# Output products of a retention and two-feed-forward kernel by seven block products, product by product over all feature rows of 768 tokens, with weight sums read back from DRAM

## The chip, the cores and the metric

The kernel runs on one core of a Trainium2 chip. The metric is the device time of one execution in microseconds. The median of three runs of the kernel before is 873.28 us (871.96 to 876.17). TensorE (PE) does the matrix products, VectorE (DVE) and ScalarE (ACT) the elementwise work, GpSimd (POOL) a little at the start, and SyncE (SP) issues every DMA, in the order of the program, on one queue.

## The reference, cut to what matters

```python
def _attn_ref(q, k, v):                      # (4, 8, 576, 64) each
    scores = scale * np.matmul(q, k.transpose(0, 1, 3, 2))
    ...
    return np.matmul(scores * Dmat[None, :, :, :], v)      # Dmat: gamma ** (i - j), i >= j
def _moe_ref(x, w_in, w_out):                # x (2304, 512), w_in (512, 2048), w_out (2048, 512)
    h = x @ w_in
    g = np.maximum(h, 0.0) + np.log1p(np.exp(-np.abs(h)))
    return g @ w_out
def _moe2_ref(x, w_in, w_out):               # same shapes
    h = x @ w_in
    r = np.maximum(h, 0.0)
    return (r * r) @ w_out
# reference: x = _attn_ref(q, k, v) as (2304, 512); x = _moe_ref(x, moe weights); _moe2_ref(x, moe2 weights)
```

Everything is float32. The kernel splits each operand of a product into a high and a low part of a shorter type (fp32r) and adds three products: high by high, low by high, high by low.

## The kernel before, in words

**First phase.** Attention runs in chunks of 64 tokens; its output is the input of the first feed-forward part, in five token tiles (TILES: 512, 384, 512, 512, 384 tokens). For each tile there are 16 steps f, one for each 128 rows of the hidden features: `g1` (L424) makes the hidden product in 12 matmuls, `softplus_a` and `softplus_b` and `split_g` make the activation and its two parts on ACT and DVE, `g2` (L476), two steps later, adds 12 matmuls into four accumulators. The result is stored to DRAM (`x2d`). Beside it `pump_step` takes weights through a chain: load, decode (`words`), split. First come the 32 weight tiles of this phase, then `split_s`: for each of 8 pairs p of the second part's input weights it makes seven block sums (two parts each) and stores them to DRAM (`s2d`) by four calls of `store_s`. That is nine steps a pair, 72 in all, spread over tiles 1 to 3. The second part's output weights (16 tiles, `split_w`) stay in SBUF; they are pumped in the last tile and the start of the second phase.

**Second phase.** Three blocks b of 768 tokens, each in two halves of 384. For a pair p of hidden row blocks the hidden product is made by seven block products (Winograd's form of Strassen's scheme): `product` (L568) makes each in 6 matmuls of 384 columns, its weights from a ring of five slots that one DMA of 256 KB each fills from `s2d`. The sums s1, u2, u3 and the four results are taken from PSUM by ACT and DVE between products; `finish` squares the positive part and splits it. The output products are plain: `piece` (L587) takes 128 tokens and one hidden row block in 3 matmuls of 512 columns, and six accumulators gather them over all pairs. `after(k)` puts one or two pieces behind each product, so each evacuation of a product's PSUM has the pieces and the next product beside it.

A tile scheduler sets the order on each engine from these calls; it may move an instruction ahead of others that don't depend on it.

Of the kernel before, what the change touches and what calls it, by code (L numbers as in the profile page):

```python
# [7 lines left out]
F32 = mybir.dt.float32  # L8
# [25 lines left out]
T_SLOTS = 10  # L34
S_SLOTS = 5
# [7 lines left out]
def kernel(  # L43
# [66 lines left out]
    s2d = dram.tile([NP, 7, P, 2, KH * P], F32, name="s2d")  # L110

# [66 lines left out]
    def store_s(p, first, src):  # L178

        n = src.shape[1] // (KH * P)  # L180
        h, l = (new_ct(F32R)[:, :n * KH * P] for _ in range(2))
        nc.scalar.copy(h, src)
        nc.vector.tensor_tensor(out=l, in0=src, in1=h, op=ALU.subtract)
        for part, o in enumerate((h, l)):
            nc.sync.dma_start(
                out=s2d[p, first:first + n, :, part].rearrange("o p c -> p o c"),
                in_=o.bitcast(F32).rearrange("p (o c) -> p o c", o=n),
            )

    def split_s(p):  # L190
# [9 lines left out]
        store_s(p, A11, top)  # L200
        yield
        store_s(p, A22, a22)
# [7 lines left out]
        store_s(p, S3, bot)  # L210
        yield
        store_s(p, S2, top)
# [17 lines left out]
    order = [f for p in range(NP // 2) for f in (p,)] + [NP, NP + 1]  # L230
    for p in range(2, NP):
        order += [p + NP] + ([p + 2] if p < NP - 2 else [])
    for f in order:
        items.append((1, split_w, (1, "wo", f)))
        loads.append((w2_out, "wo", f))
# [262 lines left out]
    def second_buffers():  # L498

        for i in range(LOADS):  # L500
            mem["ch", i] = at.tile([P, 4, HALF], F32, tag="ch", name="raw")
        mem["s"] = xs.tile([P, 4, 2, KH * P], F32R, tag="xr", name="sring")
        mem["s4"] = cvt.tile([P, 2, KH * P], F32R, tag="ct", name="sring")
# [8 lines left out]
    def s_slot(i):  # L512
        i %= S_SLOTS
        if i < 4:
            return mem["s"][:, i]
        return mem["s4"]
# [10 lines left out]
    n_s = [0]  # L527

    def load_s(upto):
        total = NB * NP * 7  # L530
        while n_s[0] < min(upto, total):
            i = n_s[0]
            nc.sync.dma_start(out=s_slot(i).bitcast(F32), in_=s2d[i // 7 % NP, PRODUCTS[i % 7]])
            n_s[0] += 1
# [24 lines left out]
    def product(b, p, k, ps, first):  # L559

        w = s_slot((b * NP + p) * 7 + k)
# [11 lines left out]
    pieces = []  # L573
    acc2 = {}

    def piece(b, p, i, j, m, g):

        h, l = g
        f = p + i * NP
        wh, wl = w_hi[1, "wo", f], w_lo[1, "wo", f]  # L580
        begin, end = p == 0 and i == j, p == NP - 1 and i != j
        if begin:
            pool, tag = (((ps_acc, "at"),) * 4 + ((ps_at, "at"), (ps_st, "st")))[j * MH + m]
            acc2[j, m] = pool.tile([P, 512], F32, tag=tag, name="acc")
        c = slice(m * P, (m + 1) * P)
# [4 lines left out]
        if end:  # L590
            t0 = b * PAIR + j * HALF + m * P
            drain_one(j * MH + m, acc2[j, m], out[t0:t0 + P, :], DM)

    n_g = [0]

    def finish(b, p, i, j, c, done=None):

        if done is None:
            g = ew.tile([P, 512], F32, tag="l", name="g")[:, :HALF]
            nc.vector.scalar_tensor_tensor(  # L600
                out=g, in0=c, scalar=0.0, in1=c, op0=ALU.max, op1=ALU.mult
            )
        else:
            g = ew.tile([P, 512], F32, tag="l", name="g")[:, :HALF]
            nc.vector.tensor_tensor(out=g, in0=done, in1=done, op=ALU.mult)
        k = n_g[0] % 4
        n_g[0] += 1
        if k < 2:
            h = gp.tile([P, 512], F32R, tag="gh", name="gh")[:, :HALF]
            l = gp.tile([P, 512], F32R, tag="gl", name="gl")[:, :HALF]  # L610
        else:
            h, l = (mem["g"][:, 2 * (k - 2) + o, :HALF] for o in range(2))
        nc.scalar.copy(h, g)  # L613
        nc.vector.tensor_tensor(out=l, in0=g, in1=h, op=ALU.subtract)
        for m in range(MH):
            pieces.append((b, p, i, j, m, (h, l)))

    def second_phase(rest):

        mem["g"] = xs.tile([P, KD, 512], F32R, tag="xh", name="gring")  # L620
        mem["u"] = xs.tile([P, KD, 512], F32, tag="xl", name="uring")
        u_ring = mem["u"].rearrange("p a b -> p (a b)")
        n_u = 0

        count = (2, 2, 2, 1, 2, 2, 1)
        skip = 5
        for b in range(NB):
            for p in range(NP):
# [5 lines left out]
                def after(k):  # L634
# [5 lines left out]
                    elif b == p == 0 and k < skip:  # L640
                        pass
                    else:
                        for _ in range(count[k]):
                            piece(*pieces.pop(0))
                    if p == 0 and k in (0, 1) and b + 1 < NB and k == 1:
                        load_raw(b + 1)
                    if b + 1 < NB and p in (3, 4, 5) and k == 2:
                        build_t((b + 1) * 7 + p - 3)
                    if b + 1 < NB and p == NP - 1 and k < 4:
                        build_t((b + 1) * 7 + 3 + k)  # L650
                    if b == 0 and k in (0, 3):
                        if n_split[0] < len(items) and not (p >= 4 and k == 3):
                            pump(1)
                    load_s((b * NP + p) * 7 + k + 1 + S_SLOTS)

                def add(a, ps):
                    c = ew.tile([P, 512], F32, tag="e", name="c", bufs=3)[:, :HALF]
                    nc.vector.tensor_tensor(out=c, in0=a, in1=ps, op=ALU.add)
                    return c

                px = h_bank("px")[:, :HALF]
# [3 lines left out]
                py = h_bank("py")[:, :HALF]  # L665
# [4 lines left out]
                r = ew.tile([P, 512], F32, tag="e", name="r", bufs=3)[:, :HALF]  # L670
                nc.scalar.activation(out=r, in_=px, func=AF.Relu)
                later.append(lambda: finish(b, p, 0, 0, None, r))
# [4 lines left out]
                pz = h_bank("pz")[:, :HALF]  # L677
                product(b, p, 4, pz, True)
                c22 = add(u3, pz)
                later.append(lambda: finish(b, p, 1, 1, c22))  # L680
                after(4)
                product(b, p, 5, py, False)
                c21 = add(s1, py)
                later.append(lambda: finish(b, p, 1, 0, c21))
                after(5)
                product(b, p, 6, pz, False)
                c12 = add(u2, pz)
                later.append(lambda: finish(b, p, 0, 1, c12))
                after(6)
        while pieces:  # L690
            piece(*pieces.pop(0))
# [116 lines left out]
    for j, (b, f) in enumerate(steps):  # L808
# [15 lines left out]
        if 1 <= b < last_b:  # L824

            total, i = 9 * NP, (b - 1) * KF + f
            while n_steps[0] < min(total, -(-total * (i + 1) // (KF * (last_b - 1) - 2))):
                pump_step()
                n_steps[0] += 1
        if b == last_b:  # L830
            if f == 0:
                assert n_split[0] == n_one + NP and not splitting
                second_buffers()
                load_raw(0)
                load_s(S_SLOTS)
            if f >= 4 and f % 2 == 0:
                pump(1)
# [6 lines left out]
    split_g(j - 1, TILES[last_b][1])  # L844
    second_phase([lambda: g2_parts(j - 2), lambda: g2_parts(j - 1)])
# [75 lines left out]
```

## Time and profile before

| | before |
|---|---|
| median of 3 runs | 873.28 us |
| profiled execution | 873.51 us |
| its span, first to last instruction | 871.7 us |
| PE, PEld (weight load), DVE, ACT busy | 852.1, 745.1, 585.0, 427.0 us |
| mean granted TensorE clock, share of 2.4 GHz | 0.989 |
| DMA | 126.34 MB, mean 145 GB/s |

The profile's page gives busy time by engine. A matmul's end is modelled and matmuls overlap, so the time that one takes in a row of them is the distance of two starts, which the chain of waits shows as the length of a piece divided by its count. The chain of waits follows the end back from wait to wait; the list of waits tells who waited for whom.

### The profile page before, as it was taken

The numbers are of one execution on the slowest core, as the hardware profiler recorded it, in microseconds if no ns is written. First come the engines' busy times: TensorE is split into PE (matmuls) and PEld (weight loads), VectorE is DVE, ScalarE is ACT, GpSimd is POOL, SyncE is SP. The second block draws the span as 40 slices with busy tenths as digits, with TensorE's granted clock in tenths as the row PEclk, the third lists the DMA queues.
The fourth block names the chain that finished last, engine by engine and source line by source line (L and its number), as shares of the span: only waits on it lengthen the run. The fifth ranks groups of instructions, "written<-read, shape, count | busy, mean of one in ns | idle before, by whom it ended". The sixth has DMA issues, their size and how long they took to land.

```text
span 871.7 us, 14325 instructions
## 1 busy us (share of the span) xinstructions
PE 852.1 (98%) x5520; PEld 745.1 (85%) x5520; DVE 585.0 (67%) x1038; ACT 427.0 (49%) x795; POOL 9.3 (1%) x12
## 2 busy tenths in 40 slices
PE   8899999999999999999999999999999999999998
PEld 6677787989888888788999989889888988998996
DVE  4689998986897578755888874446745446554444
ACT  3589998665676456744686561213312113221121
POOL 2100000000000000000000000000000000000000
PEclk9699999999999999999999999999999999999999
DMA  8856774972394116710431464436644444644342
GB/s 206 219 165 201 217 207 113 286 240 53 95 293 132 39 49 222 233 43 1 169 115 55 145 230 121 119 112 193 192 114 117 121 117 116 191 119 114 118 121 85
DMA packets 75784, 126.34 MB, mean 145 GB/s; under 512 B 6722, under 2 KB 41666, under 8 KB 75714
## 3 DMA queue, kind: packets, MB, share of 16 engines
q1 hardware_dynamic: 75716, 125.42, 49.1%
q8 instruction: 44, 0.72, 0.4%
q14 instruction: 24, 0.20, 0.1%
HBM read 101.28 MB, written 24.12 MB: 144 GB/s over the span
## 4 chain that ended last, share of the span: by engine, by line
PE 79%; DVE 7%; DMA 6%; ACT 4%; issue 2%; SPq 1%; POOL 0%; DVEq 0%; ACTq 0%
PE acc L587 23%; PE ph L424 16%; PE acc L476 16%; PE py L568 9%; PE px L568 6%; PE pz L568 6%; DMA ch<-in_kv_dram 2%; DMA wo_raw<-in_moe_w_out_dram 2%; PE po L359 2%; PE pb L330 1%; DMA s2d<-ct 1%; DVE e L451 1%; DVE l L448 1%; PE st L336 1%; DVE ct L145 1%
## 5 line engine op out<-in xcount | busy, mean ns | idle before, releaser
L424 PE MATMUL ph<-xh,wi 128*128 128x512 f32 (+1 forms) x640 | 146.0, 369 | 2.3 <-DVE e L451 1.3
L424 PEld LDWEIGHTS ph<-xh,wi 128*128 128x128 f32 x640 | 116.3, 188 | 19.8 <-DVE e L451 2.4
L476 PE MATMUL acc<-gh,woh 128*128 128x512 f32 (+1 forms) x320 | 120.2, 379 | 0.7 <-ACT gh L460 0.7
L476 PE MATMUL acc<-gh,wol 128*128 128x512 f32 (+1 forms) x320 | 118.1, 369 | 0.0
L476 PE MATMUL acc<-gl,woh 128*128 128x512 f32 (+1 forms) x320 | 117.9, 369 | 0.0
L587 PE MATMUL acc<-woh,gring 128*128 128x512 f32 x288 | 104.9, 393 | 0.0
L568 PE MATMUL py<-t,sring 128*128 128x384 f32 x432 | 86.8, 335 | 0.3 <-DVE uring L675 0.3
L568 PEld LDWEIGHTS py<-t,sring 128*128 128x128 f32 x432 | 77.2, 188 | 6.8 <-DVE uring L675 0.6
L460 ACT CAST gh<-e 128x512 fp32r<-128x512 f32 (+1 forms) x80 | 46.0, 575 | 73.3 <-DVE e L451 65.7
L424 PE MATMUL ph<-xl,wi 128*128 128x512 f32 (+1 forms) x320 | 78.7, 367 | 0.0
L445 DVE SCALAR_TENSOR_TENSOR e<-e 128x512 f32<-128x512 f32 (+1 forms) x80 | 50.9, 637 | 33.8 <-ACT l L440 32.8
L461 DVE TENSOR_TENSOR gl<-e,gh 128x512 fp32r<-128x512 f32 (+1 forms) x80 | 51.0, 637 | 31.2 <-ACT gh L460 30.5
L476 PEld LDWEIGHTS acc<-gh,woh 128*128 128x128 f32 x320 | 59.8, 188 | 9.4 <-ACT gh L460 0.8
L613 ACT CAST gh<-g 128x384 fp32r<-128x384 f32 x48 | 24.6, 513 | 87.1 <-DVE g L600 72.4
L476 PEld LDWEIGHTS acc<-gh,wol 128*128 128x128 f32 x320 | 60.1, 188 | 7.9
L476 PEld LDWEIGHTS acc<-gl,woh 128*128 128x128 f32 x320 | 60.1, 188 | 7.2 <-DVE gl L461 0.2
L613 ACT CAST gring<-g 128x384 fp32r<-128x384 f32 x48 | 24.6, 513 | 83.4 <-DVE g L600 83.4
L424 PEld LDWEIGHTS ph<-xl,wi 128*128 128x128 f32 x320 | 58.7, 188 | 7.6
L587 PEld LDWEIGHTS acc<-woh,gring 128*128 128x128 f32 x288 | 54.0, 188 | 9.2
L438 ACT ACTIVATE e<-ph 128x512 f32<-128x512 f32 (+1 forms) x80 | 44.2, 552 | 33.2 <-PE ph L424 32.7
L568 PE MATMUL px<-t,sring 128*128 128x384 f32 x288 | 58.3, 337 | 0.0
L568 PE MATMUL pz<-t,sring 128*128 128x384 f32 x288 | 58.2, 337 | 0.0
(79 smaller groups left out, 1458.4 us busy)
## 6 DMA issues: line engine op xcount, KB each, us to landing
sring<-s2d SPq DMA_DIRECT2D x168, 256.0 KB, 2.7
wi_raw<-in_moe_w_in_dram SPq DMA_DIRECT2D x32, 512.0 KB, 4.5
wo_raw<-in_moe_w_out_dram SPq DMA_DIRECT2D x32, 512.0 KB, 4.6
s2d<-ct SPq DMA_DIRECT2D x48, 256.0 KB, 3.1
ch<-in_qk_t_dram SPq DMA_DIRECT2D x36, 256.0 KB, 4.6
ch<-in_kv_dram SPq DMA_DIRECT2D x36, 256.0 KB, 4.9
raw<-x2d SPq DMA_DIRECT2D x12, 384.0 KB, 3.3
out_dram<-xo SPq DMA_DIRECT2D x18, 256.0 KB, 2.2
```

What stands on the lines that cost most here:

```text
L145: nc.vector.scalar_tensor_tensor(out=ct, in0=up, scalar=3, in1=low, op0=ALU.logical_shift_left, op1=ALU.bitwise_or,)
L330: nc.tensor.matmul(pb[to, h, :], lhsT=kk[LO, hh, :], rhs=qp[LO, hh, :], start=True, stop=True, skip_group_check=True,)
L359: nc.tensor.matmul(po[(LO, HI)[h % 2], h // 2, :], lhsT=sv[rows, h, :], rhs=qp[rows, h, :], start=True, stop=True, skip_group_check=True,)
L424: nc.tensor.matmul(ph[:, :n], lhsT=a, rhs=x, start=(j == 0), stop=(j == len(todo) - 1))
L438: nc.scalar.activation(out=e, in_=ph[:, :n], func=AF.Abs)
L445: nc.vector.scalar_tensor_tensor(out=e, in0=e, scalar=-2.0, in1=e, op0=ALU.add, op1=ALU.mult)
L460: nc.scalar.copy(h[:, :n], g)
L461: nc.vector.tensor_tensor(out=l[:, :n], in0=g, in1=h[:, :n], op=ALU.subtract)
L476: nc.tensor.matmul(acc[j][:, :n], lhsT=a, rhs=x, start=(begin and m == 0), stop=(end and m == 2))
L568: nc.tensor.matmul(ps, lhsT=a, rhs=x, start=(first and m == 0), stop=(m == len(todo) - 1), skip_group_check=True,)
L587: nc.tensor.matmul(acc2[j, m], lhsT=a, rhs=x, start=(begin and n == 0), stop=(end and n == 2))
L613: nc.scalar.copy(h, g)
```

## The change

The second phase's output products are made by seven block products too. The 768 tokens by 2048 features of a block are one operand, the 16 output weight tiles the other; the blocks are the two token halves, the feature halves (p and p + 8) and the two halves of the 512 outputs. A block b now runs in two parts. First come all hidden products of the eight pairs, one behind the other, each evacuated into a buffer for all features (`g_slot`, in the space of the first phase's weights). Then come 56 units, product by product over all eight p: `split_unit` makes the operand (a sum or difference on DVE for four of the seven products) and its two parts three units ahead (AHEAD), `unit` runs 9 matmuls of 256 columns, and after the eighth unit of a product its sum is taken from PSUM.

The output weights' sums are made in the first phase by `split_o` (eight pairs, nine steps each) and stored to a new DRAM tensor `o2d`. The steps of both splits, 144, are spread over tiles 1 to 4 instead of 72 over tiles 1 to 3. The ring has ten slots; each unit loads one 256 KB tile from `o2d`, as each product does from `s2d`.

```diff
-T_SLOTS = 10
-S_SLOTS = 5
+T_SLOTS = 8
+S_SLOTS = 10
+AHEAD = 3
+O_PRODUCTS = (0, 3, 1, 4, 6, 2, 5)
...
+    def split_o(p):
+        cts = []
+        for f in (p, p + NP):
+            t = staged.pop(("wo", f))
+            cts.append(new_ct())
+            yield from words(t, cts[-1])
...
+        store_s(o2d, p, 0, a11)
+        yield
+        store_s(o2d, p, 1, bot)
+        yield
+        nc.vector.tensor_tensor(out=a22, in0=a21, in1=a22, op=ALU.add)
...
+        store_s(o2d, p, 3, top)
+        yield
+        store_s(o2d, p, 5, bot)
+        yield True
...
-    for f in order:
-        items.append((1, split_w, (1, "wo", f)))
-        loads.append((w2_out, "wo", f))
+    for p in range(NP):
+        items.append((2, split_o, (p,)))
+        loads += [(w2_out, "wo", p), (w2_out, "wo", p + NP)]
...
+        in_order += [s2d[p, k] for p in range(NP) for k in PRODUCTS]
+        in_order += [o2d[p, k] for k in O_PRODUCTS for p in range(NP)]
...
-        for n, (a, x) in enumerate([(h[:, c], wh), (h[:, c], wl), (l[:, c], wh)]):
-            nc.tensor.matmul(
-                acc2[j, m], lhsT=a, rhs=x, start=(begin and n == 0), stop=(end and n == 2)
-            )
...
+    def split_unit(u):
+        k, p = units[u]
+        g11, g12, g21, g22 = (g_slot(p, i, j) for i in range(2) for j in range(2))
+        t2 = g_extra(p)
+        if k == 1:
+            minus(t2, g22, g11)
+        elif k == 5:
+            minus(g21, g21, t2)
+        src = (g11, t2, g21, g12, g11, g21, g22)[k]
...
+        nc.scalar.copy(h, src)
+        minus(l, src, h)
+        if k == 0:
+            minus(g11, g12, g11)
+        elif k == 2:
+            minus(g12, g22, g12)
+        pairs[u] = h, l
...
+        for m in range(MH):
+            c = slice(m * P, (m + 1) * P)
+            for n, (a, x) in enumerate([(h[:, c], w[:, 0]), (h[:, c], w[:, 1]), (l[:, c], w[:, 0])]):
+                nc.tensor.matmul(
+                    blocks[m], lhsT=a, rhs=x, start=(first and p == n == 0 and m in opens),
+                    stop=(p == NP - 1 and n == 2), skip_group_check=True,
+                )
...
+            split_unit(u + AHEAD)
+            unit(b, u, blocks, tiles, k in where)
+            load_s((2 * b + 1) * NP * 7 + u + 1 + S_SLOTS)
...
-                    else:
-                        for _ in range(count[k]):
-                            piece(*pieces.pop(0))
...
-            total, i = 9 * NP, (b - 1) * KF + f
-            while n_steps[0] < min(total, -(-total * (i + 1) // (KF * (last_b - 1) - 2))):
+            total, i = 18 * NP, (b - 1) * KF + f
+            while n_steps[0] < min(total, -(-total * (i + 1) // (KF * last_b - 4))):
                 pump_step()
```

The order on PE in the second phase, before (px, py, pz are the PSUM tiles of the hidden products, t their operand, sring the weight ring; acc are the output accumulators, gh and gl or gring the two parts of the activation, woh and wol those of the output weights):

```order
L568 MATMUL px<-t_4821,sring 128x384 [waits DMAHW5_49,Activation_49]
L568 MATMUL px<-t_4821,sring 128x384 x5
L587 MATMUL acc<-woh_5493,gring 128x512
L587 MATMUL acc<-wol_5494,gring 128x512
L587 MATMUL acc<-woh_5493,gring 128x512 x2
L587 MATMUL acc<-wol_5494,gring 128x512
L587 MATMUL acc<-woh_5493,gring 128x512
L568 MATMUL py<-t_4821,sring 128x384 [waits DMAHW6_49,DVE_49]
```

The same place after, and two units of the second part (there px, py and pz are the sums of the output products):

```order
L613 MATMUL pz<-t_5219,sring 128x384 [waits DMAHW2_49]
L613 MATMUL pz<-t_5219,sring 128x384 x5
L613 MATMUL py<-t_5219,sring 128x384 [waits DMAHW3_49,DVE_49]
L613 MATMUL py<-t_5219,sring 128x384 x5
L613 MATMUL pz<-t_5348,sring 128x384 [waits DMAHW4_49,DVE_49]
```

```order
L678 MATMUL px<-sring,gh 128x256 [waits DMAHW5_49,Activation_49]
L678 MATMUL px<-sring,gh 128x256
L678 MATMUL px<-sring,gl 128x256 [waits DVE_49]
L678 MATMUL px<-sring,gh 128x256 x2
L678 MATMUL px<-sring,gl 128x256
L678 MATMUL px<-sring,gring 128x256 [waits DMAHW6_49,Activation_49]
```

The pieces no longer stand between the hidden products; one product of 6 matmuls stands between a product and the next one that writes the same PSUM tile, and a unit waits for a DMA, for ACT and for DVE.

The order on DVE at the last pair (p = 7) of a block's hidden products, before (L667 makes u2, L675 u3, L605 the square of the first result, L557 the low part of the next block's operand t):

```order
L614 TENSOR_TENSOR gring<-g,gring 128x384 [waits Activation_49]
L557 TENSOR_TENSOR t_4693<-raw,t_4693 128x768 [waits PE_49,Activation_49]
L667 TENSOR_TENSOR uring<-uring,py 128x384 [waits PE_49,Activation_49]
L557 TENSOR_TENSOR t_4693<-raw,t_4693 128x768 [waits Activation_49]
L557 TENSOR_TENSOR t_4821<-raw,t_4821 128x768 [waits PE_49,Activation_49]
L605 TENSOR_TENSOR g<-r 128x384 [waits Activation_49]
L675 TENSOR_TENSOR uring<-uring,py 128x384 [waits PE_49]
```

After (L791 makes u2, L797 u3, L778 the square, L602 the next block's operand, L767 a result):

```order
L602 TENSOR_TENSOR t_4926<-raw,t_4926 128x768 [waits PE_49,Activation_49]
L791 TENSOR_TENSOR uring<-uring,py 128x384 [waits PE_49,Activation_49]
L602 TENSOR_TENSOR t_4926<-raw,t_4926 128x768 [waits DMAHW4_49,Activation_49]
L602 TENSOR_TENSOR t_5078<-raw,t_5078 128x768 [waits PE_49,Activation_49]
L778 TENSOR_TENSOR g<-r 128x384 [waits Activation_49]
L797 TENSOR_TENSOR uring<-uring,py 128x384 [waits PE_49]
L602 TENSOR_TENSOR t_5078<-raw,t_5078 128x768 [waits Activation_49]
L767 TENSOR_TENSOR g<-uring,pz 128x384 [waits DVE_49,PE_49]
```

The builds of the next block stand in the same place, ahead of u2 and u3, while the pieces that stood beside them on PE are gone.

## Rows read from the trace of the kernel before

**Rows 1.** The page: busy us (share of the span) and instructions of each engine.
```profile
PE 852.1 (98%) x5520; PEld 745.1 (85%) x5520; DVE 585.0 (67%) x1038; ACT 427.0 (49%) x795; POOL 9.3 (1%) x12
```

**Rows 2.** Busy time by stretch: first phase's tiles 1 and 2, and the second phase.
```profile
core 0: us, PE busy (x) PEld busy (x) DVE busy (x) ACT busy (x) POOL busy (x), PEclk, DMA share, GB/s
138.00:222.30 84.30, 80.81 (x754) 75.97 (x753) 69.16 (x137) 54.99 (x111) 0.00 (x0) 1.00 0.55 164
222.30:319.80 97.50, 97.50 (x754) 79.85 (x753) 75.60 (x134) 59.30 (x105) 0.00 (x0) 1.00 0.45 130
...
740.00:862.00 122.00, 122.00 (x607) 109.55 (x606) 58.75 (x106) 24.67 (x49) 0.00 (x0) 1.00 0.43 121
```

**Rows 3.** The chain of waits in the second phase: start us, us, what.
```profile
642.09 1.06 PE px L568 x6
643.15 1.39 PE acc L587 x6
644.54 1.04 PE py L568 x6
...
861.01 4.14 PE acc L587 x18
```

**Rows 4.** Groups by shape on PE: count | busy us, mean ns | idle before, releaser.
```profile
L587 PE MATMUL acc<-woh,gring 128*128 128x512 f32 x288 | 104.9, 393 | 0.0
...
L568 PE MATMUL py<-t,sring 128*128 128x384 f32 x432 | 86.8, 335 | 0.3 <-DVE uring L675 0.3
...
L568 PEld LDWEIGHTS py<-t,sring 128*128 128x128 f32 x432 | 77.2, 188 | 6.8 <-DVE uring L675 0.6
```

**Rows 5.** Waits of PE from 138 to 482 us: us in total, times, longest.
```profile
PE pb L330 <- DVE e L451: 3.3, 5, 1.4
...
PE ph L424 <- DVE ch L341: 0.3, 1, 0.3
```

**Rows 6.** Timeline at 51.7 us, after a wait of PE: start us, us, instruction.
```profile
51.72 0.19 PEld L476 LDWEIGHTS acc<-gh,woh 128*128 128x128 f32 x1
51.73 0.50 PE L476 MATMUL acc<-gh,woh 128*128 128x512 f32 x1
51.83 0.19 PEld L476 LDWEIGHTS acc<-gl,woh 128*128 128x128 f32 x1
...
52.06 0.39 PE L476 MATMUL acc<-gl,woh 128*128 128x512 f32 x1
```

**Rows 7.** Timeline: a product's evacuation, PE's wait for one, two DVE operations.
```profile
707.13 1.21 PE L568 MATMUL py<-t,sring 128*128 128x384 f32 x6
...
708.44 0.56 DVE L667 TENSOR_TENSOR uring<-uring,py 128x384 f32<-128x384 f32 x1 [1.90 <-PE py L568]
...
495.87 0.55 DVE L675 TENSOR_TENSOR uring<-uring,py 128x384 f32<-128x384 f32 x1
...
496.47 1.31 PE L568 MATMUL py<-t,sring 128*128 128x384 f32 x6 [0.29 <-DVE uring L675]
...
498.33 1.02 DVE L600 SCALAR_TENSOR_TENSOR g<-c 128x384 f32<-128x384 f32 x2
```

**Rows 8.** Groups by shape on DVE, from 482 us on.
```profile
L614 DVE TENSOR_TENSOR gl<-g,gh 128x384 fp32r<-128x384 f32 x48 | 26.8, 558 | 24.1 <-ACT gh L613 24.1
...
L557 DVE TENSOR_TENSOR t<-raw,t 128x768 fp32r<-128x768 f32 x13 | 12.5, 958 | 4.2 <-ACT t L556 4.0
```

**Rows 9.** Busy time by stretch as in rows 2; last two columns DMA share, GB/s.
```profile
497.00:507.00 10.00, 10.00 (x52) 9.03 (x51) 7.85 (x17) 6.27 (x12) 0.00 (x0) 1.00 0.95 348
...
640.00:700.00 60.00, 60.00 (x300) 53.98 (x299) 26.85 (x50) 11.54 (x23) 0.00 (x0) 1.00 0.43 119
```

**Rows 10.** DMA issues of the weight ring: count, KB each, median us to landing.
```profile
sring<-s2d SPq DMA_DIRECT2D x168, 256.0 KB, 2.7
```

**Rows 11.** The chain of waits at the end of the span.
```profile
865.89 2.04 DMA out_dram<-xo
...
868.04 0.69 DVE xo L486
```

More of the change, by code (lines that the diff above doesn't have):

```diff
@@ L185, in store_s @@
             nc.sync.dma_start(
-                out=s2d[p, first:first + n, :, part].rearrange("o p c -> p o c"),
+                out=to[p, first:first + n, :, part].rearrange("o p c -> p o c"),
                 in_=o.bitcast(F32).rearrange("p (o c) -> p o c", o=n),
@@ L502, in second_buffers, with more_buffers @@
         mem["s"] = xs.tile([P, 4, 2, KH * P], F32R, tag="xr", name="sring")
-        mem["s4"] = cvt.tile([P, 2, KH * P], F32R, tag="ct", name="sring")
+    def more_buffers():
+        for i in range((S_SLOTS - 4) // 2):
+            mem["s", i] = stage.tile([P, 2, 2, KH * P], F32R, tag="st", name="sring")
+        for s in range(NP * 5):
+            f, part = divmod(s, 2)
+            if f < KF:
+                pool = wts if f < EARLY["wo"] else late_wts[0]
+                tag = f"wo{'hl'[part]}{f}"
+                mem["g", s] = pool.tile([P, 512], F32, tag=tag, name="g")[:, :HALF]
+        wide = late_wts[0].tile([P, 8, HALF], F32, tag="wi4", name="g")
+        for s in range(2 * KF, NP * 5):
+            mem["g", s] = wide[:, s - 2 * KF]
+        mem["o"] = xs.tile([P, KD, 512], F32R, tag="xh", name="gring")
+        mem["u"] = xs.tile([P, KD, 512], F32, tag="xl", name="uring")
     def raw(i, j):
@@ L611, in finish @@
         else:
-            h, l = (mem["g"][:, 2 * (k - 2) + o, :HALF] for o in range(2))
-        nc.scalar.copy(h, g)
-        nc.vector.tensor_tensor(out=l, in0=g, in1=h, op=ALU.subtract)
-        for m in range(MH):
-            pieces.append((b, p, i, j, m, (h, l)))
+            h, l = (mem["o"][:, 2 * (r - 2) + o, :HALF] for o in range(2))
+        nc.scalar.copy(h, src)
[4 more added lines that the diff above has]
+            minus(g12, g22, g12)
@@ new lines, in split_unit, with sums, unit @@
+        pairs[u] = h, l
+    def sums(name, where):
+        blocks, tiles = [], []
+        for n, (pool, tag) in where:
+            t = pool.tile([P, 512], F32, tag=tag, name=name)
+            tiles.append((t[:, :n * KH * P], len(blocks), n))
+            blocks += [t[:, m * KH * P:(m + 1) * KH * P] for m in range(n)]
+        return blocks, tiles
+    def unit(b, u, blocks, tiles, first):
+        k, p = units[u]
+        h, l = pairs.pop(u)
+        w = s_slot((2 * b + 1) * NP * 7 + u)
+        opens = [at for _, at, _ in tiles]
+        for m in range(MH):
+            c = slice(m * P, (m + 1) * P)
[4 more added lines that the diff above has]
+                )
```

193 lines of the change are left out of this document (117 added, 76 removed).

## The prediction

> **What bounds the kernel now.** I read the busy time by engine first: PE has 852.1 of 871.7 us [rows 1]. That alone says little, since a matmul's end is modelled, so I went to busy time by stretch: in the second phase PE has 122.00 of 122.00 us at a granted clock of 1.00 (the 2.4 GHz level), DVE 58.75 and ACT 24.67 [rows 2]. The chain of waits there holds nothing but matmuls back to back, product (L568) and pieces (L587) in turn [rows 3], and in the whole phase PE waited once, 0.3 us [rows 4]. So there the time is the number of matmuls times the distance of their starts. The reader should take that distance from the chain: six matmuls of 512 columns fill 1.39 us and eighteen fill 4.14 us, 0.230 to 0.232 each; six of 384 columns fill 1.04 to 1.06 us, 0.173 to 0.177 each [rows 3]. I use 0.231 and 0.176. There are 864 of the first kind (one group of 288 and four of 144) and 1008 of the second (432, 288, 288) [rows 4]. 864 x 0.231 + 1008 x 0.176 = 199.6 + 177.4 = 377 us; with some 4 us for the last stores [rows 11] that leaves about 490 us for the first phase. The first phase is another matter: in tile 1 PE has 80.81 of 84.30 us and DVE 69.16 [rows 2], and all PE's waits are for DVE, 5.6 us in four groups from 138 to 482 us, of which rows 5 show the first and the last.
>
> **The output products.** The change takes out the 864 pieces and puts in 3 blocks x 56 units x 9 = 1512 matmuls of 256 columns; columns fall from 442,368 to 387,072, seven eighths. The trace before has no full-size matmul of 256 columns, so I bound its distance. From 512 to 384 columns it falls by 0.231 - 0.176 = 0.055 us; another 128 columns less gives 0.176 - 0.055 = 0.121 us. That holds if streaming columns still sets it. Every matmul also loads its own 128x128 weights, recorded at 188 ns [rows 4]. That can't be the load's hold on the array, for six matmuls with six such loads take 1.04 us, 0.173 each [rows 3]. The rows that show more stand at 51.7 us: after a wait two loads start 0.11 us apart, and the matmul of the first is drawn 0.11 us too long (0.50 against 0.39), so it really began about when the second load did [rows 6]. A load thus needs 0.11 us until its matmul can start, and the next load starts with that matmul. 0.11 is under 0.121, but by little. The lower bound is 0.116 (the same straight line through 0.230 and 0.173), the upper one 0.188, the recorded load. I take 0.121, near the rows of loads 0.11 us apart, because they alone show a load that waits for no matmul: 1512 x 0.121 = 183.0 us, **16.6 us less** than 199.6 (24 less to 85 more at the bounds).
>
> The Trainium skill has a rule against this. "TensorE: Matmul & The Clock Gate", part 3, what overlaps and what doesn't, says that a weight load runs beside a running matmul only where the two use different row groups; here all rows are in use, so load and stream would add up, and by it the units would take about 349 us, 150 more than the pieces. The trace does not agree: 384 columns alone stream 0.055 x 3 = 0.165 us, and with the load's 0.11 six would take 1.65 us, where the chain has 1.04 [rows 3].
>
> **The hidden products without pieces between them.** Their 1008 matmuls stay, 177.4 us. What goes is cover. Today the pieces and one product lie between a product and the next writer of its PSUM tile; now one product does, 6 x 0.176 = 1.06 us. The evacuation's way: the product at 707.13 starts its last matmul at 708.01 (1.21 less that matmul's 0.335), DVE starts at 708.44 and takes 0.56; at 496 us DVE ended at 496.42 and PE's load started at 496.47 [rows 7]. 0.43 + 0.56 + 0.05 = 1.04 us, against 1.06 plus the 0.07 us by which a matmul's distance exceeds its load: 0.09 us to spare. Queued on DVE between these evacuations are squares and, from p = 5 on, the first units' parts; two operations back to back take 1.02 us [rows 7], 0.51 each, and some ten of them in a pair of 7.4 us leave room. I take zero; if each of three tight waits in 24 pairs ran 0.05 us over, it would be 3.6 us. At p = 7 of blocks 0 and 1 builds of 0.958 us [rows 8] stand ahead of u2 and u3 on DVE; before, pieces covered them. PE has seven unit matmuls (0.85 us) to put before u3's wait and little before u2's. Each block loses between 0 and 2 x 0.96 us; I take the middle, 1 us each, **2 us more**.
>
> **The units.** Nine matmuls are 9 x 0.121 = 1.09 us of PE. Beside them stand one cast on ACT and one operation of 0.558 us on DVE [rows 8], two in four of the seven products: 1.02 us when back to back [rows 7]. There DVE keeps up by 0.07 us a unit, and in the other three products by 0.5, where builds and PSUM sums go; three units of lead hide unevenness. If each operation pays its whole 0.558 and 0.03 us of waiting for ACT, two are 1.18 us, 0.09 over, 32 times a block: 2.9 us, 8.6 in all. Between 0 and 8.6 I take **1.5 us more**, near the low end, because the order on DVE has runs of these operations side by side, like the pair in rows 7.
>
> **The DMAs.** Each product and each unit needs one 256 KB tile, 336 instead of 168, on SP's queue: 88 MB, and with x2d and the outputs (8 MB) 96 MB in some 362 us, 265 GB/s. The second phase now moves 119 GB/s at a share of 0.43, but 348 GB/s went through for ten microseconds at 0.95 [rows 9]. A ring of ten slots issues loads nine products ahead, some 9.5 us, against 2.7 us to landing [rows 10]. An output store on SP's queue that waits for DVE holds the loads behind it for about a microsecond, which that lead covers. I cost this at nothing; without that cover it is the third rival.
>
> **The weight sums.** Eight `split_o`, 72 steps, replace 16 `split_w`, and tiles 1 to 4 get 2.4 split steps per f where tiles 1 to 3 had 1.57. In tile 1 that is 1.5 pairs more; a pair is two decodes, four splits and four sums on DVE, ten operations of about 0.56 us, so DVE goes from 69 to some 77 of 84 us [rows 2]. The 64 stores (14.7 MB) wait on SP's queue for ACT and DVE, with attention's loads queued behind them. If PE's waits grow with this work, 5.6 us [rows 5] x 2.4 / 1.57 = 8.6, that is 3 more, and 1 for tile 4, where the ring's slots 4 to 9 wait for the last split. It could be 0, if the softplus chain has slack, or 9, if the waits of tile 1 treble. **4 us more**, and **1 us more** (0 to 4) for the entry into the second phase, whose first loads queue behind the last stores.
>
> **The end.** Today the last copy waits for a store of 2.04 us to free its buffer [rows 11]. Now the last sums go to a pool of six buffers: **1.3 us less** (0 to 2).
>
> **The sum** is against the profiled execution, 873.5 us (its span 871.7 and 1.8 around it; the median of the runs is 873.3): 873.5 - 16.6 + 2 + 1.5 + 4 + 1 - 1.3 = **864.1 us**.
>
> **The rivals.**
> *Waits eat it.* The distance is 0.121 but DVE is late: first phase 9, units 8.6, evacuations 3.6, p = 7 4, entry 4. All of them give 873.5 - 16.6 + 29 - 1.3 = 885; the forecast's 8.5 and half of the excess give 874. For it: DVE near nine tenths in tile 1. Against: 0.3 us of waits in the second phase so far.
> *The load sets the distance* (slower). Place: every matmul of a unit. If a load's hold grows when loads follow each other at this pace, the distance lies between 0.121 and 0.188 us. From 199.6 / 1512 = 0.132 us on the gain is gone; at 0.15 us units take 226.8 us and the time is 873.5 + 27.2 + 7.2 = 908, at 0.188 us 965. Against: the 0.11 us of rows 6, which show two loads in a row, though, and never a stream.
> *DMA sets the pace* (slower). It decides from under 265 GB/s on. At a share of 0.43 for 119 GB/s [rows 9] a full share would be 277; if only 245 came through, 96 MB take 392 us, 30 more: about 894. Against: 348 GB/s for ten microseconds.
> *Load and stream add*, 0.11 + 0.121 = 0.231 us a matmul, 349 us for the units: 873.5 + 150 + 7 = 1030 us. The six matmuls in 1.04 us speak against it. This is what the skill's sentence above would make of the kernel.
>
> **How the numbers follow.** The forecast, 855 to 869 us, gets 0.67; waits eat it, 869 to 879, 0.14; the load 0.10; DMA 0.06; load and stream adding 0.01; 0.02 is left below 855. A measurement of this kernel can tell about 0.5% from no change, so 869.1 to 877.9 us counts as the same. Faster is the forecast and the tail below it, 0.69; within 0.5% nearly all of the second case, 0.13; slower the rest, 0.18. The range runs from 854 (0.118 us and few waits) to 879 and leaves out the load, DMA and the adding, 0.17, and a little of the tail.
>
> **What would show it.** Right: 1512 matmuls of which nine take about 1.09 us in the chain; hidden products with 1.04 to 1.06 us for six and no wait between them but at p = 7; a DMA share near 0.8; PE's waits from 138 to 482 us near 9 us. Wrong: unit matmuls 0.13 us apart or more with gapless loads beside them; PE waiting for sring's DMAs; waits for DVE at every unit of a product with two operations.

## The result, and the profile of the changed kernel

The changed kernel takes 860.41 us (median, 858.34 to 861.18); the kernel before takes 873.77 us beside it (871.96 to 876.17). The ratio is 0.9842, with a 95% interval of 0.9812 to 0.9872: faster by 1.6%. The forecast was 864.1 us. The profiled execution took 860.06 us with a span of 858.3, 13.4 less than the 871.7 of before.

The page of the changed kernel, busy time by engine (it answers rows 1) and the loads of the ring (rows 10):

```profile
PE 837.6 (98%) x6168; PEld 765.6 (89%) x6168; DVE 685.9 (80%) x1277; ACT 468.1 (55%) x886; POOL 9.0 (1%) x12
...
sring<-s2d SPq DMA_DIRECT2D x168, 256.0 KB, 3.2
sring<-o2d SPq DMA_DIRECT2D x168, 256.0 KB, 3.5
```

PE's share is 98% as before, which again says little. DVE has 100 us more to do, and little of that is on the path in the second phase. The chain of waits there (start us, us, what) answers rows 3 and, with its last lines, rows 11:

```profile
506.33 1.06 PE py L613 x6
507.39 1.04 PE pz L613 x6
508.43 1.04 PE py L613 x6
...
563.80 8.96 PE py L678 x72
572.76 8.72 PE px L678 x72
581.48 8.64 PE py L678 x72
...
626.48 1.14 PE py L613 x6
...
673.71 1.28 PE py L613 x6
...
846.25 8.65 PE pz L678 x72
854.90 0.02 issue
854.92 0.42 DVE xo L707
```

Each piece of 72 matmuls is one product over all eight p, eight units of nine. 8.64 / 72 = 0.120 us a matmul, and 17 of the 19 whole pieces in the chain are 8.63 to 8.65 us long. Most hidden products follow each other every 1.04 to 1.06 us; 17 of them take 1.10 to 1.32 us, as those at 626.48 and 673.71. From start to start these delays add up to 1.8 us. The list of PE's own waits is empty from 500 us to the end, but that of its weight loads (PEld) is not:

```profile
PEld py L613 <- DVE uring L791: 0.7, 3, 0.3
PEld px L613 <- ACT uring L787: 0.5, 2, 0.2
PEld py L613 <- DVE uring L797: 0.3, 2, 0.2
```

Busy time by stretch (columns as in rows 2), for tiles 1, 2 and 3 of the first phase and a stretch of the second, and ahead of them tile 3 of the kernel before:

```profile
319.80:416.30 96.50, 95.61 (x626) 77.58 (x625) 67.09 (x115) 54.25 (x94) 0.00 (x0) 1.00 0.37 118
...
138.00:222.30 84.30, 82.29 (x755) 77.55 (x753) 72.83 (x147) 59.59 (x120) 0.00 (x0) 0.98 0.73 215
222.30:322.20 99.90, 98.92 (x752) 80.65 (x753) 84.29 (x155) 66.37 (x120) 0.00 (x0) 1.00 0.56 175
322.20:421.90 99.70, 96.02 (x626) 77.54 (x625) 75.65 (x134) 61.99 (x109) 0.00 (x0) 1.00 0.53 164
...
740.00:850.00 110.00, 110.00 (x777) 109.46 (x776) 84.88 (x166) 36.51 (x73) 0.00 (x0) 1.00 0.81 254
```

PE has 110.00 of 110.00 us beside gapless weight loads (109.46), DVE 84.88, and the DMAs move 254 GB/s at a share of 0.81. Tile 1 takes the 84.3 us that it took before (with a granted clock of 0.50 for 3.4 us of it); tile 2 takes 99.9 instead of 97.5, tile 3 99.7 instead of 96.5. DVE's work grows by 3.7 us in tile 1, by 8.7 in tile 2 and by 8.6 in tile 3. PE's waits from 138 to 490 us (us in total, times, longest), for rows 5:

```profile
PE pb L357 <- DVE e L478: 5.3, 7, 1.5
PE ph L451 <- DVE e L478: 1.5, 2, 0.8
PE ph L451 <- DVE xl L422: 0.3, 1, 0.3
PE ph L451 <- DVE ch L368: 0.3, 1, 0.3
```

**Where the 13.4 us came from.** The last first-phase matmul starts at 492.7 us before and 497.9 us after, 5.2 later. From there to the end it is 379.0 us before and 360.4 after, 18.6 less: 18.1 in the output products (from start to start the 1512 matmuls take 182.0 us, against 200.1 for the 864 before; all pieces of L678 in the chain add up to 181.8), and 0.6 at the end (last matmul's start to the end of the span 4.28 us before, 3.68 after). The hidden products behind that point take the same in all, to 0.1 us.

### The profile page after: what moved, and what is told of

It is laid out like the page before. It is cut to its first block, busy times and chain, and to the rows that moved or that the text cites. A ratio compares the mean times of both kernels' runs of the same rounds, so it can differ in the third digit from the quotient of the medians.

```text
span 858.3 us, 16848 instructions
## 1 busy us (share of the span) xinstructions
PE 837.6 (98%) x6168; PEld 765.6 (89%) x6168; DVE 685.9 (80%) x1277; ACT 468.1 (55%) x886; POOL 9.0 (1%) x12
## 4 chain that ended last, share of the span: by engine, by line
PE 68%; DVE 11%; ACT 9%; DMA 8%; issue 2%; SPq 1%; POOL 0%; ACTq 0%; DVEq 0%
PE acc L503 12%; PE ph L451 12%; PE py L678 9%; PE py L613 9%; PE px L678 6%; PE pz L678 6%; PE px L613 6%; PE pz L613 6%; DMA wo_raw<-in_moe_w_out_dram 2%; DVE e L478 2%; DVE ct L187 2%; DMA s2d<-ct 1%; DVE l L475 1%; DMA wi_raw<-in_moe_w_in_dram 1%; DMA ch<-in_kv_dram 1%
## 5 line engine op out<-in xcount | busy, mean ns | idle before, releaser
L613 PEld LDWEIGHTS py<-t,sring 128*128 128x128 f32 x432 | 75.3, 188 | 2.1 <-DVE uring L791 0.7
L653 ACT CAST gh<-g 128x384 fp32r<-128x384 f32 x84 | 43.0, 513 | 46.8 <-PE px L678 16.7
L653 ACT CAST gring<-g 128x384 fp32r<-128x384 f32 x84 | 43.2, 514 | 42.7 <-PE py L678 18.2
L639 DVE TENSOR_TENSOR gring<-g,gring 128x384 fp32r<-128x384 f32 x84 | 46.7, 556 | 18.4 <-ACT gring L653 16.4
L639 DVE TENSOR_TENSOR gl<-g,gh 128x384 fp32r<-128x384 f32 x84 | 46.3, 556 | 18.7 <-ACT gh L653 18.4
L787 ACT COPY uring<-px 128x384 f32<-128x384 f32 x24 | 11.5, 479 | 87.7 <-PE px L613 87.7
## 6 DMA issues: line engine op xcount, KB each, us to landing
sring<-s2d SPq DMA_DIRECT2D x168, 256.0 KB, 3.2
sring<-o2d SPq DMA_DIRECT2D x168, 256.0 KB, 3.5
s2d<-ct SPq DMA_DIRECT2D x48, 256.0 KB, 3.4
o2d<-ct SPq DMA_DIRECT2D x48, 256.0 KB, 3.0
ch<-in_qk_t_dram SPq DMA_DIRECT2D x36, 256.0 KB, 5.1
ch<-in_kv_dram SPq DMA_DIRECT2D x36, 256.0 KB, 5.1
```

Of the source, the lines that this page charges most:

```text
L613: nc.tensor.matmul(ps, lhsT=a, rhs=x, start=(first and m == 0), stop=(m == len(todo) - 1), skip_group_check=True,)
L639: nc.vector.tensor_tensor(out=out, in0=a, in1=b, op=ALU.subtract)
```

## The experiments

### What sets the distance of the unit matmuls

**half_columns** streams half of each unit matmul's columns.

```diff
+                cols = KH * P if first and p == n == 0 else KH * P // 2
-                    blocks[m], lhsT=a, rhs=x, ...
+                    blocks[m][:, :cols], lhsT=a, rhs=x[:, :cols], ...
```

> The unit matmuls run on 128 of their 256 columns, all but the opening one of each product (left out: half of the output products' columns). My theory, a weight load holds the next matmul for 0.11 us: the distance of two starts stops at 0.108 to 0.112 us, the 1449 short ones save 1449 x 0.010 = 14 us at most, and less where DVE, with two operations a unit, cannot follow at 0.99 us a unit. Rival, the load costs nothing of its own and only columns count: the distance falls to about 0.067 us (one more 0.054 step down from 0.120), a unit needs 0.6 us of PE, and PE waits for DVE in most units, so that the time falls by 20 to 40 us and the chain goes to DVE.

Measured: 991.66 us, 131 slower than the changed kernel. The timeline (start us, us, instruction) and the windows tell why:

```profile
556.71 2.09 PEld L679 LDWEIGHTS px<-sring,gring 128*128 128x128 f32 x18
556.77 2.17 PE L679 MATMUL px<-sring,gring 128*128 128x128 f32 x18
...
600.97 2.25 PEld L679 LDWEIGHTS py<-sring,gring 128*128 128x128 f32 x10
...
560.00:564.00 4.00, 2.73 (x20) 2.26 (x19) 3.26 (x8) 3.00 (x6) 0.00 (x0) 1.00 0.93 293
...
600.00:655.00 55.00, 55.00 (x259) 55.00 (x260) 18.26 (x34) 13.80 (x27) 0.00 (x0) 0.50 0.54 156
660.00:720.00 60.00, 59.75 (x334) 58.83 (x333) 46.96 (x87) 12.95 (x25) 0.00 (x0) 0.97 0.81 246
```

At 556.71 the granted clock is 1.00 (2.4 GHz) and a load is recorded at 0.19 us; 18 loads take 2.09 us, so they start (2.09 - 0.19) / 17 = 0.112 us apart, with half the columns. That is the load's hold that rows 6 showed in one pair, here in a row of eighteen. Nine such matmuls are 1.01 us, no more than two DVE operations back to back (1.02 us, [rows 7]), and from 561 us on PE waits for DVE and ACT: from 560 to 564 us it is busy for 2.73 of 4.00 us. At 564.5 us the granted clock falls to 0.50 (1.2 GHz), and ten loads of 0.33 us take 2.25: (2.25 - 0.33) / 9 = 0.213 us apart, nearly twice as long. It then stays there, though PE and its loads are busy for 55.00 of 55.00 us. The clock is back at 663.5 us, when the next block's hidden products (384 columns) run, and falls again in the next units (at 731.8 us, after PE was busy for 2.03 of 3.80 us). So the load's hold is a floor of 0.112 us at 2.4 GHz, and the changed kernel's 0.120 stands 0.008 above it. Most of the 131 us are the stretches at 0.50, 96 to 100 us in each block.

**columns_192** does the same with 192 of 256 columns (`KH * P * 3 // 4`).

> As half_columns, with 192 of the 256 columns in every unit matmul but the opening one of a sum, so a quarter of the output products is left out. Stream alone would be 0.120 - 0.027 = 0.093 us, the load's hold at the 2.4 GHz level was 0.107 in half_columns. If the load's hold is a floor: 0.107 to 0.110 us a unit matmul while the granted clock is 1.00, 1512 x 0.013 = 20 us less than the changed kernel, 840 us, if the clock stays. If matmuls that are shorter than the load's hold bring the clock down as in half_columns, stretches at 0.50 with 0.21 us a matmul, up to 990 us. If the floor is not there: 0.093 to 0.097, near 825 us.

Measured: 870.25 us in one run. The median distance of two starts is 0.111 us at a clock of 1.00, where streaming alone would give 0.093: the floor again, as the first theory said, at 0.112 rather than the 0.107 that it names for half_columns. The 840 us that it drew from this didn't come. The granted clock fell to 0.50 only for 10.2, 6.8 and 3.4 us around the three first products, each time after waits of PE, which was busy for 1.89 of 3.60, 1.95 of 3.90 and 2.06 of 3.80 us before the falls. PE now waited from 500 us on; the first line shows fourteen loads in a row, (1.65 - 0.19) / 13 = 0.112 us apart:

```profile
719.83 1.65 PEld L679 LDWEIGHTS py<-sring,gring 128*128 128x128 f32 x14
...
PE px L679 <- DVE gring L639: 5.9, 5, 1.6
PE py L679 <- DVE gl L639: 1.8, 2, 1.0
```

Nine matmuls at 0.111 are 1.00 us, less than the 1.02 us of two DVE operations back to back [rows 7]. A quarter of the columns less gains nothing: streaming alone would give 1512 x 0.027 = 41 us, the load's floor takes two thirds of it (1512 x 0.018 = 27 us), and DVE and the clock take more than the rest. How much of that falls to each of the two was not separated.

### How much cover DVE has

**dve_third_op** writes each unit's low part twice.

```diff
         minus(l, src, h)
+        minus(l, src, h)
```

> Each unit's low part is written twice on DVE, so a unit has two DVE operations in three products and three in four. My account has DVE at 0.48 to 0.56 us an operation beside 1.08 us of PE a unit: three are 1.43 to 1.68 us, 0.35 to 0.6 over, 32 times in each of three blocks, less the lead of three units, and the other products catch up little: 25 to 55 us more than the changed kernel, 885 to 915 us, with PE waiting for DVE in the units of four products and in no others. Rival, DVE has more room than that, since no wait of a unit shows in the changed kernel: under 5 us more.

Measured: 873.04 us in one run, 12.6 more than the changed kernel, with these waits from 500 us on:

```profile
PE py L679 <- DVE gl L639: 3.5, 8, 0.8
PE py L679 <- DVE gring L639: 3.0, 3, 1.0
```

168 more operations of 0.549 us are 92 us; only 12.6 came out, in the profile 16.0 after the last first-phase matmul and 3.1 less before it. In products with one operation the second fits, and in those with two the third runs into PE's 1.08 us. The expectation was too high. Back to back DVE starts such operations every 0.47 us (two take 1.02, [rows 7]); by that three would be 0.33 over, 32 us in 96 units. That the lead of three units carries the rest on into the next product is argued and not shown.

### How much cover the loads have

**ring_of_4** and **ring_of_6** change one size.

```diff
-S_SLOTS = 10
+S_SLOTS = 4
```

> The weight ring has four slots instead of ten, nothing else. A load is issued three products ahead, 3.2 us at 1.06 us a product, and the tiles of the changed kernel take 3.2 to 3.5 us to land. If the lead is the cover, as I costed it, PE waits a few tenths of a us for sring's DMAs at most of the 336 tiles: 20 to 80 us more than the changed kernel, about 880 to 940 us. Rival, the DMA engines' rate alone decides and a load in flight is enough: no change, 860 us.

Measured: 914.12 us (908.26 to 916.18), ratio to before 1.0443 (1.0403 to 1.0482). PE waits for ring tiles, from 500 us on, 27.3 us in all; the three longest:

```profile
PE py L678 <- DMA sring<-o2d: 9.0, 8, 2.0
PE pz L678 <- DMA sring<-o2d: 6.6, 6, 2.1
PE px L678 <- DMA sring<-o2d: 5.1, 9, 1.0
```

> Six slots instead of ten: a load is issued five products ahead, 5.3 us against 3.2 to 3.5 us to landing. If landing time against lead is what counts: within 3 us of the changed kernel, 858 to 864 us. Rival, the lead has to cover bursts too (operand loads of 384 KB each and output stores on the same queue): 5 to 15 us more, with PE's waits at those places.

Measured: 866.11 us (861.62 to 869.16), ratio 0.9901 (0.9866 to 0.9935), 5.7 more than the changed kernel: outside the theory's range and at the low end of the rival's. In its profile 4 us of the longer span lie in the first phase (last matmul at 501.9 us), although the order on DVE and ACT is the changed kernel's, so this part scatters by some us between executions; the other 5 lie behind it, where PE waits 2.1 us for ring tiles. Six slots are nearly enough. Four are not: their lead of three products, 3.1 us, is about the landing time.

**dma_plus_quarter** and **dma_plus_half** put a second transfer, from DRAM to DRAM, beside each ring tile.

```diff
             nc.sync.dma_start(out=s_slot(i).bitcast(F32), in_=in_order[i])
+            nc.sync.dma_start(
+                out=spare[i % 16].rearrange("a b c -> a (b c)"),
+                in_=in_order[i][:64].rearrange("(a b) o c -> a (b o c)", b=2),
+            )
```

> Beside each of the 336 ring tiles a DMA of 64 KB goes from DRAM to DRAM, a quarter more to move: 22 MB, 118 MB in the second phase, 328 GB/s over 359 us. My theory, the DMA engines hold up to 348 GB/s: time within 3 us of the changed kernel, 858 to 864 us, at a DMA share over 0.9. Rival, they were at their bound already (share 0.8 to 0.9 at 250 GB/s): the second phase grows with the bytes, 20 us or more, over 880 us, and PE waits for sring's DMAs.

> The same with 128 KB beside each ring tile: 44 MB more, 140 MB, which at 348 GB/s take 402 us against 359 of PE. My theory: the DMA engines are the bound now, about 40 us more than the changed kernel, 885 to 915 us, with PE waiting for sring's DMAs. Rival, DRAM to DRAM transfers are much cheaper for the engines than loads into SBUF: less than 10 us more.

The pages list these transfers with 128.0 and 256.0 KB, twice what the expectations name, so the moved bytes grew by a half and by the whole. Measured: 903.84 us (901.95 to 905.98), ratio 1.0346 (1.0312 to 1.038), and 938.18 us in one run. The first looks as if the DMA engines had no margin. Its SyncE timeline spoke for something else: issues in a row, 0.57 us apart. So I took the bytes out and left the transfers.

**two_kb_beside_ring** is the same edit with one row of `spare` (4 KB by the page's count).

> The changed kernel with a transfer of 2 KB from DRAM to DRAM beside each of the 336 ring tiles (dma_plus_half's code with 2 KB in the place of 128 KB). Its order on PE, DVE and ACT is that of dma_plus_half to the last instruction; it differs from the changed kernel's in where the block sums' additions and casts stand among the attention and softplus work of tiles 2 to 4. In the profiles of dma_plus_quarter and dma_plus_half the last hidden product of the first phase started at 486.5 and 484.4 us, 4 to 6 us earlier than the changed kernel's 490.6, with the same instructions. Theory: the weight sums' price of 6.4 us (from no_output_sums) is mostly the place on DVE and ACT that the scheduler gave them, not their work; so 854 to 858 us, last first-phase hidden product near 485. Rival: those two profiles were early by chance, or the larger transfers moved something; then 859 to 862 us.

Measured: 897.97 us (896.39 to 900.93), ratio 1.028 (1.0254 to 1.0307), far from both theories; nearly the whole loss of dma_plus_quarter without its bytes. The timeline of SyncE's queue:

```profile
640.53 0.53 SPq L579 DMA_DIRECT2D sring<-s2d  x1
641.10 0.47 SPq L580 DMA_DIRECT2D spare<-s2d  x1
641.67 0.53 SPq L579 DMA_DIRECT2D sring<-s2d  x1
642.24 0.47 SPq L580 DMA_DIRECT2D spare<-s2d  x1
642.81 0.53 SPq L579 DMA_DIRECT2D sring<-s2d  x1
```

In this alternation an issue comes every 0.57 us whatever its size, a pair every 1.14, and PE takes a hidden product every 1.04 to 1.06 and a unit every 1.08. So SyncE set the pace for long stretches. The Trainium skill says in "Perfetto Trace Analysis", section What "DMA-bound" means, that a kernel can be bound by the sequencer of the engine that issues, whose track is then solid DMA slices, and that such a slice is the making of descriptors and not the movement of data; this trace agrees, with issues of 0.47 to 0.53 us in every 0.57 and 228 GB/s (640 to 700 us). The 44 MB of dma_plus_quarter then cost 903.8 - 898.0 = 6 us, at 325 GB/s and a share of 0.96 in the same stretch. Only dma_plus_half shows the DMA engines full, 396 GB/s at 1.02. In the changed kernel an issue of a ring tile alone is recorded at 0.32 us, one for each product or unit of 1.04 to 1.08 us, at 254 GB/s; where two stand in a row and don't wait, they start 0.41 to 0.51 us apart (553 to 575 us).

### What the weight sums cost

**no_output_sums** takes `split_o` out and spreads 72 steps as before; the units read `s2d`.

```diff
-    for p in range(NP):
-        items.append((2, split_o, (p,)))
...
-        in_order += [o2d[p, k] for k in O_PRODUCTS for p in range(NP)]
+        in_order += [s2d[p, k] for k in O_PRODUCTS for p in range(NP)]
```

> The output weights' sums are neither loaded, decoded, split nor stored; the units read the input weights' sums in their place (left out: the output weights), and the first phase's split steps are again 72 over tiles 1 to 3. The second phase is untouched. My theory, the sums in the first phase cost about 5 us there and nothing else did: 855 to 857 us, the last hidden product of the first phase starting near 482 us instead of 489. Rival, the first phase's 6 us come from the order and the buffers, not from the amount of work: 860 us again. Rival, the second phase is slowed by stores of the sums too: under 853 us.

Measured: 853.97 us (851.69 to 854.61), ratio 0.9757 (0.9734 to 0.978). With the sums out, 6.4 us are gone; the last first-phase matmul starts at 492.0 us instead of 497.9, and the second phase is unchanged (0.120 us a unit matmul). But PE's waits from 138 to 490 us are 5.5 us there and 7.4 in the changed kernel, only 1.9 more beside 6.4 us of time. The edit also changes the order of what is left on DVE, so this run alone doesn't tell the sums' work from their place.

**scale_on_pool** gives one attention operation of each chunk in the tiles to GpSimd.

```diff
-                scale_v(c - 1 + LOADS)
+                scale_v(c - 1 + LOADS, nc.gpsimd)
```

> The scaling of attention's v (0.69 us of DVE, 19 times in tiles 1 to 3) goes from DVE to POOL, which is idle there; all else is as in the changed kernel. If the first phase's waits come from DVE being full in tiles 1 to 3: 13 us less work on DVE there, PE's waits from 138 to 482 us fall from 7 to 3 us or so, 856 to 858 us. Rival, POOL is slower at it or its result comes too late for the chunk: same time or a few us more.

Measured: 861.59 us (860.66 to 863.42), ratio 0.9864 (0.9833 to 0.9894): no gain. The last first-phase matmul starts at 497.9 us as before the edit, and PE's waits from 138 to 490 us rose from 7.4 to 9.1 us.

**sums_on_pool** gives the additions of both splits to GpSimd.

```diff
-        nc.vector.tensor_tensor(out=a22, in0=a21, in1=a22, op=ALU.add)
+        nc.gpsimd.tensor_tensor(out=a22, in0=a21, in1=a22, op=ALU.add)
...
```

> The changed kernel with the eight additions of each pair of block sums (four for the input weights, four for the output weights) on GpSimd, which is idle there, instead of DVE. They stand in no chain that PE waits for. Theory that DVE's load sets the first phase's price: DVE loses some 30 us of busy time in tiles 1 to 4, PE's waits for DVE from 138 to 490 us fall from 7.4 to under 4, 855 to 858 us. Rival: an addition takes longer on GpSimd than on DVE and slows DVE beside it, or it moves the order as much as it saves: 859 to 864 us.

Measured: 873.97 us (872.54 to 876.87), ratio 1.0003 (0.9983 to 1.0023), 13.6 more than the changed kernel and beyond the rival. DVE lost work, yet PE's waits for it from 138 to 505 us rose to 20 us. Groups on DVE from 138 to 490 us (count | busy us, mean ns | idle before), of this kernel:

```profile
L187 DVE TENSOR_TENSOR ct<-ct 128x512 fp32r<-128x512 f32 x48 | 34.0, 711 | 16.3 <-ACT ct L186 15.7
L475 DVE SCALAR_TENSOR_TENSOR l<-e,l 128x512 f32<-128x512 f32 x33 | 24.0, 728 | 0.8
...
L478 DVE SCALAR_TENSOR_TENSOR e<-ph,l 128x512 f32<-128x512 f32 x33 | 22.7, 689 | 0.8
```

and of the changed kernel:

```profile
L187 DVE TENSOR_TENSOR ct<-ct 128x512 fp32r<-128x512 f32 x48 | 32.9, 686 | 4.1 <-ACT ct L186 4.0
...
L475 DVE SCALAR_TENSOR_TENSOR l<-e,l 128x512 f32<-128x512 f32 x33 | 22.7, 688 | 0.5
L478 DVE SCALAR_TENSOR_TENSOR e<-ph,l 128x512 f32<-128x512 f32 x33 | 22.7, 688 | 0.5
```

An addition takes 0.42 us on DVE and 0.73 to 1.07 (medians by line) on GpSimd. The sums come later, ACT's cast of them too, and DVE stands 16.3 us instead of 4.1 before the low part (L187), with the softplus chain queued behind it. DVE's operations on two SBUF operands become longer (L475, 688 to 728 ns), the one that reads PSUM doesn't (L478). The Trainium skill says in "GPSIMD Engine Reference", section 1, Specifications, that GpSimd shares its SBUF interfaces with VectorE and contends with instructions with two SBUF inputs; those rows agree. How much each of the two gives was not separated.

**order_of_sums.** The three kernels with spare transfers ended their first phase 3 to 6 us early (last matmul at 492.1 to 494.9 us instead of 497.9), though they do the same work there: the scheduler had given the sums' operations other places. This kernel keeps that order on DVE and ACT with 56 small transfers.

```diff
+            if 224 <= i < 280:
+                nc.sync.dma_start(
+                    out=spare[i % 16][:1].rearrange("a b c -> a (b c)"),
+                    in_=in_order[i][:2].rearrange("(a b) o c -> a (b o c)", b=2),
+                )
```

> The changed kernel with a small transfer from DRAM to DRAM (4 KB by the page's count; the runs before this one named half the size that the page shows, 128 and 256 KB in dma_plus_quarter and dma_plus_half, 4 KB in two_kb_beside_ring) beside only the 56 hidden ring tiles of the last block. In the first phase its order on PE is that of two_kb_beside_ring, on DVE and ACT nearly so (30 and 8 rows of difference), while the changed kernel's differs from it by some 460, 230 and 16 rows: the scheduler puts the block sums' additions and casts at other places among attention and softplus. In two_kb_beside_ring 336 more issues on SP's queue cost some 41 us in the second phase, 1.14 us for an issue of each kind against 1.06 us of PE; 56 of them fall short by 0.08 to 0.13 us each, 4.5 to 7 us, which the ten slots' lead of some 9 us covers, so 0 to 2 us. Theory (the place of the sums is worth some 4 us: first hidden product to last one of the first phase 450.8 us in the changed kernel, 445.6 to 448.2 in the three profiles of the other order): 446 to 449 us from the first to the last hidden product of the first phase, 856 to 859 us in all. Rival (the difference is scatter between executions of the first phase): 449 to 453, 860 to 863 us.

Measured: 855.12 us (854.26 to 857.68), ratio 0.9773 (0.9747 to 0.9799), 5.3 less than the changed kernel and the fastest that does the whole work. From the first to the last hidden product of the first phase it took 446.0 us (39.7 to 485.7) against 450.8, as the theory had it; the whole is 0.9 us under its range. PE's waits in tile 3 of the changed kernel,

```profile
PE pb L357 <- DVE e L478: 2.7, 2, 1.4
PE ph L451 <- DVE e L478: 0.7, 1, 0.7
PE ph L451 <- DVE ch L368: 0.3, 1, 0.3
```

and of this one:

```profile
PE pb L358 <- DVE e L479: 0.7, 1, 0.7
```

Tile 3 takes 96.1 us instead of 99.7, tile 2 98.1 instead of 99.9, with DVE busy in tile 3 for 75.48 us here and 75.65 there. At one pair in tile 2, for instance, three of the additions stand one softplus operation earlier on DVE, the last of them and a sum's low part ahead of an attention operation and of the low part of the activation. That this is no scatter the other profiles show: the six with the changed kernel's order on DVE take 449.4 to 454.2 us from the first to the last hidden product of the first phase, the four with this order, but for a few rows, 445.7 to 448.2. So of the 6.4 us the order that the scheduler gave to DVE costs 5.3. The 855.12 - 853.97 = 1.2 us that are left for the sums' work lie within the noise of the two runs (0.9747 to 0.9799 against 0.9734 to 0.978). Which operations in that order PE's chain pays for was not separated; a few of attention's matmuls on PE moved too.

## Why the prediction was right

**The distance** was the step that mattered. The straight line through 512 and 384 columns gave 0.121 us [rows 3]; it is 0.120. Units take 182.0 us, where 183.0 was forecast. The near floor of 0.11 us [rows 6] is real, 0.112 (half_columns, columns_192), and was rightly taken as lying just below. Both rivals on the load fall: the recorded 188 ns is no hold even in a gapless stream, and load and stream don't add. The Trainium skill's rule that a load runs beside a matmul only in other row groups ("TensorE: Matmul & The Clock Gate", part 3) would have asked for 349 us; the trace of after has 182.0.

**The hidden products** were costed at nothing for their evacuations, with 0.09 us to spare. That was a little too good: in pairs 1 to 4 of blocks 1 and 2 one product each starts 0.07 to 0.1 us late, behind DVE's u2 (L791). The 2 us at p = 7 were mis-sized: three hidden products and a unit matmul there lose 0.4 us a block, 0.8 in all, since the unit matmuls that PE can put there cover most of both builds. What these delays cost came back elsewhere: a product behind a piece took 1.06 us, one behind a product takes 1.04 [rows 3].

**The units' 1.5 us** are 0.4, in the pieces of 8.96 and 8.72 us of the first block. Two operations back to back and three units of lead hold the pace, and dve_third_op shows how much more fits.

**The DMAs** at nothing: right, and 254 GB/s at a share of 0.81 is near the 265 and 0.8 that were forecast. That ten slots are the cover is shown by ring_of_4; that bytes have room, by dma_plus_quarter beside two_kb_beside_ring. The rival looked at bytes and left out the nearer limit, SyncE's issues, 0.57 us each when every ring tile has a second transfer beside it.

**The weight sums and the entry**, 4 + 1 us, measured 5.2 in the profile and 6.4 by no_output_sums. The size was right; the step to it was not. It let PE's waits grow with DVE's work and saw tile 1 as the place, with DVE at 77 us. DVE came to 72.83 there and tile 1 lost nothing; the new work lay in tiles 2 and 3, and they lost 5.6 us. But order_of_sums has the same work on DVE there and loses little, so most of the price was the order in which the scheduler put the sums among softplus and attention. That the size fitted was luck.

**The end** was forecast at 1.3 us less and gave 0.6: the store's wait is gone, but a sum and a last store remain.

The sum came out 4 us high (864.1 against 860.1 in the profiled execution): the units with their waits took 182.0 us and not 183.0 + 1.5, the hidden products took no more than before where 2 were added, and the pieces before had taken 200.1 and not 199.6; against these 5 us stand 0.7 that the end came short and 0.2 more in the first phase.

## What to carry to other kernels

Before matmuls are made narrower, read the weight load's own distance from a place where two loads follow each other after a wait: down to that distance a narrower matmul gains in proportion, below it nothing, and here PE then ran ahead of DVE, waited, and lost the clock. Price added transfers by the issue slots of the queue that issues them as well as by their bytes, and price added work on an engine by the place it gets ahead of the chain that the matmuls wait for: the same sums cost 6.4 us in one order and some 1.2, hardly above the noise, in another.

## What was not expected of the hardware

In half_columns the granted clock fell to 0.50 after PE had waited for DVE and ACT (2.73 of 4.00 us busy), and it stayed there for 96 to 100 us a block while 128-column matmuls and their loads kept PE busy without a gap (55.00 of 55.00 us); the load's hold went from 0.112 to 0.213 us with it. With 256 columns it stayed at 1.00 through the changed kernel's second phase. And where ring tiles and small transfers alternate, one of 4 KB holds SyncE's queue as long as one of 256 KB, 0.57 us from issue to issue (two_kb_beside_ring).
